# Turning q and k of the second batch on TensorE in a top-k attention + MLP kernel, where they were turned by DMA

## The chip, the cores and the metric

The kernel runs on one core of one Trainium2 chip. The metric is device time in microseconds, from the start of the program to its end; smaller is better. A measurement is the median of several runs.

## What is computed

Attention over 8 batches of 8 heads, 576 rows of 64 values each, in float32, in which every row keeps only its 32 largest scores; then a two-layer MLP with a sigmoid-gated activation on the result. Cut to what matters:

```python
# q, k, v: (8, 8, 576, 64)
scores = (1 / sqrt(64)) * q @ k.T                  # (576, 576) for each head
kth = np.partition(scores, -32)[..., -32:-31]
scores = np.where(scores >= kth, scores, -1e9)
attn = softmax(scores)                             # over the kept ones
attn_out = attn @ v                                # (8, 8, 576, 64)
x = attn_out.transpose(0, 2, 1, 3).reshape(4608, 512)
h = x @ w_in                                       # (4608, 2048)
g = h * sigmoid(1.702 * h)
out = g @ w_out                                    # (4608, 512)
```

## The kernel before

**Slots.** The unit of attention work is a slot: 128 query rows of a pair of heads (`hp`, 0 to 3). A head has 576 = 4 x 128 + 64 rows, so a batch has 16 full slots, and two more ("ends") that put the last 64 rows of two head pairs together: 18 slots a batch, 144 in all. Slots 0 to 17 are batch 0; slot 18 is the first of batch 1, which the kernel's text calls `b == 1` and this document "the second batch". Slots 18, 19, 20 and 21 are the first to need the q and k of its head pairs 0, 1, 2 and 3.

**What one slot does.** TensorE computes the scores (`scores`, L283). ScalarE copies them scaled from PSUM to SBUF (`copy_scores`, L295). VectorE pairs the two halves of each row (`pair_up`, L324; GpSimd makes the complement, L327 and L328), and finds the 32nd largest (`topk_of_pairs`, max and match-replace, L345 and L348): this document calls it "the find". GpSimd forms a bound (`lows`, L378). ScalarE applies the threshold (L398) and the exponential (L401). The probabilities must then be turned, and this is done by DMA: ScalarE splits the float32 words into their two 16-bit halves (`split`, L471), a DMA writes them to DRAM (L473), and a transposing DMA brings them back turned (`turn_by_dma`, L479, tile `pt`). TensorE multiplies with v (`values_at`, L539), ScalarE copies the result out of PSUM (L921) and GpSimd divides by the sum of the row (`x_of`, L553), which TensorE has turned (`sum_rows`, L528).

**The MLP beside it.** As soon as the four head pairs of 128 rows are done, the rows are appended to `ready`. Four hidden steps (`hidden`, L587, 32 matmuls each), each with a tanh on ScalarE (L604) and a gate on GpSimd (L616, L617), and four projection steps (`project`, L635, 8 matmuls each) make the output of 128 rows; ScalarE takes it from PSUM (L641, tile `ob`) and a DMA stores it. A projection of the next rows needs `ob` to have been read out. Tanh results and `ob` share five buffers.

**What sets the order.** Nothing is scheduled by a planner: the program order is written by hand, each engine executes its part of it strictly in order, and semaphores between the engines come from the tiles. Slots 0 to 12 are issued by `slot(n)`; from slot 13 on `two_slots(n)` issues two slots at a time, n = 13, 15, 17 and so on ("pair 13", "pair 15"). Work that is due at a slot is entered by `at(slot, function, arguments)` (L682 to L686) and taken up there: loads and v at the beginning of each half of a pair (`begin`), preparations of q and k at a fixed place in each half (`prepare_some`, L898 and L936). SyncE's queue (SP) issues nearly all DMAs, also in program order: a DMA that waits for its data holds up all that follow it.

In pair n, TensorE's order is: a hidden step and a projection (if there is something to do), then at L902 the turned sums of slots n-3 and n-2, scores of n+2, values of n-3 and n-2, scores of n+3 (in pair 13 the first of these come at other places), then a second hidden step and projection. ScalarE's order is: exponentials and split of slot n-1; tanh; scores of n+2; the first half of the exponentials of n, the copy L921, the second half; split of n; scores of n+3; tanh; `ob` where due. VectorE does the finds of n and n+1. The find of slot n contains, after 14 of its steps, `pair_up(n+1)`, which needs the copied scores of n+1.

**How q and k get turned.** q and k are loaded with rows on partitions (`load_both`: six DMAs to a tile `qk_l`, two buffers) and are needed with the 64 values of a head on partitions (tile `qk_t`, six buffers). There are two ways in the kernel:

- `prepare` (L210), used for batch 0: for q, four 128 x 128 transposes on TensorE (L218) into one PSUM bank (tile `tp`, two buffers, which the hidden steps and the results of `values_at` use in turn too), and a ScalarE copy of 128 x 512 (L219); for k the same, and one more transpose for the 64 last rows of both (L222) with three ScalarE copies of 128 x 64 (L223, L225).
- `prepare_by_dma` (L236), used for batches 1 to 7: a ScalarE copy that splits all words into 16-bit halves (L241, 128 x 2304; the tile `halves` takes a buffer of the probabilities' pool), four DMAs that write them to DRAM (L245, twice, L249, L250), and a transposing DMA (L254) that brings them back. That last one isn't issued at once: it is put into the list `turns`, which `two_slots` works off just behind `turn_by_dma(n - 1)` (L911).

Where the second batch is fetched and prepared is set by two tables, counted from slot 18:

```python
    READY_1 = (-5, -4, -2, -1)      # slots 13, 14, 16, 17
    FETCH_1 = (-11, -9, -4, -3)     # slots 7, 9, 14, 15
```

Of the kernel before, what the change touches and what calls it, by code (L numbers as in the profile page):

```python
# [30 lines left out]
def kernel(  # L31
# [238 lines left out]
    PER = N // B  # L270
    st = [{} for _ in slots]

    def scores(n):
        b, t, hps = slots[n]
        ps = [ps_s.tile([P, 2, 512], F32, name="s_ps") for _ in range(2)]
        if t < NF:
            parts = [(i, 0, slice(0, P), slice(t * P, (t + 1) * P)) for i in range(2)]
        else:
            parts = [(i, p, slice(p * TAIL, (p + 1) * TAIL), slice(FULL, S)) for i, p in ((0, 0), (1, 1), (0, 1), (1, 0))]
        for c in range(2):  # L280
            for i, p, rows, cols in parts:
                on = slice(i * D, (i + 1) * D)
                nc.tensor.matmul(  # L283
                    ps[i][rows, c, 0:HALF],
                    lhsT=qT[b, hps[p]][on, cols],
                    rhs=kT[b, hps[p]][on, FIRST[i] + c * HALF : FIRST[i] + (c + 1) * HALF],
                )
        st[n]["ps"] = ps
# [93 lines left out]
    def bounds(n):  # L382

        if n >= PAIRED:
            return lows(n)
        top = st[n]["top"]
        cut = st[n]["cut"] = small.tile([P, 2], F32, name="cut")
        low = st[n]["low"] = small.tile([P, 2], F32, name="low")
        nc.gpsimd.tensor_scalar(cut[:], top[:, :, TOPK - 1], -1.0, None, op0=ALU.mult)  # L389
        nc.gpsimd.tensor_tensor(out=low[:], in0=top[:, :, TOPK - 1], in1=top[:, :, 0], op=ALU.subtract)  # L390
# [34 lines left out]
    def invert(n):  # L425

        k = n // 2
        if k in sums:
            total = sums[k][:]
            nc.vector.tensor_scalar_add(total, total, 1e-9)  # L430
            inverse = small.tile([P, 4], F32, name="inverse")
            nc.vector.reciprocal(inverse[:], total.rearrange("p s j -> p (s j)"))
            wide = sums[k] = raws.tile([P, 2, 2, D], F32, name="wide", tag="raw")
            nc.gpsimd.tensor_copy(
                out=wide[:].rearrange("p s j d -> p (s j) d"),
                in_=inverse[:].unsqueeze(2).to_broadcast([P, 4, D]),
            )
# [29 lines left out]
    def split(n):  # L467

        pr, sc = st[n]["pr"], st[n]["sc"]
        halves = sc[:].rearrange("p i k -> p (i k)").bitcast(U16).rearrange("p (h k) -> p h k", h=2)  # L470
        nc.scalar.copy(out=halves, in_=pr[:].bitcast(U16).rearrange("p (k h) -> p h k", h=2))  # L471
        rows = st[n]["rows"] = apart.tile([P, 2, 2 * S], U16, name="rows")
        nc.sync.dma_start(rows[:], halves)  # L473
# [137 lines left out]
    def gate(aside):  # L611
        if not gated:
            return
        th, h, g, rows = gated.pop(0)
        if aside:
            nc.gpsimd.tensor_scalar(th[:], th[:], 1.0, 1.0, op0=ALU.add, op1=ALU.mult)  # L616
            nc.gpsimd.tensor_tensor(out=th[:], in0=th[:], in1=h[:], op=ALU.mult)  # L617
        else:
            nc.vector.scalar_tensor_tensor(
                out=th[:], in0=th[:], scalar=1.0, in1=h[:], op0=ALU.add, op1=ALU.mult  # L620
            )
        to_project.append((th, g, rows))

    def project(put_off_leaving=False):

        gT, fs, rows = to_project.pop(0)
        if fs.start == 0:
            pos[:] = [
                home.tile([P, C], F32, name="po", tag=tag) for home, tag in ((ps_p, "po"), (ps_h, "ph"))[: len(rows)]
            ]  # L630
        blocks = iter(range(G))
        for f in fs:
            for po in pos:
                i = next(blocks)
                nc.tensor.matmul(  # L635
                    po[:], lhsT=gT[:, i * P : (i + 1) * P], rhs=wout[:, f, :], start=(f == 0), stop=(f == FC - 1)
                )
        if fs.stop == FC:
            def leave(po, to_rows):
                ob = thp.tile([P, C], F32, name="ob", tag="th")  # L640
                nc.scalar.mul(out=ob[:], in_=po[:], mul=0.5 / RAISE**2)  # L641
                for on, to in to_rows:
                    nc.sync.dma_start(to, ob[on, :])

            leaving.extend(lambda po=po, to=to: leave(po, to) for po, to in zip(pos, rows))
            if not put_off_leaving:
                leave_all()
# [10 lines left out]
    def at(n, fn, *args):  # L658
        later.setdefault(n, []).append((fn, args))
# [2 lines left out]


    READY = (-13, -11, -5, -3)
    READY_1 = (-5, -4, -2, -1)
    FETCH = (-17, -15, -9, -7)
    FETCH_1 = (-11, -9, -4, -3)
    VALUES = (0, 1, 2, 3)
    by_slot = dict(enumerate([2, 2, 3, 3, 3, 3, 3, 3, 3, 3, 2, 2]))
    for n in by_slot:  # L670
# [11 lines left out]
    for b in range(1, B):  # L682
        for hp in range(NP):
            at(b * PER + (FETCH if b > 1 else FETCH_1)[hp], load_both, b, hp)
            at(b * PER + (READY if b > 1 else READY_1)[hp], prepare_by_dma, b, hp)
            at(b * PER + VALUES[hp], load_v, b, hp)  # L686
    unfinished = []
    early = []
# [2 lines left out]
    def finish_one():  # L691
        unfinished.pop(0)()

    def may_project(waiting):

        return len(to_project) > waiting and len(finished) >= NG * CC + to_project[0][1].stop
# [62 lines left out]
    def bring_all():  # L759

        waiting = len(ready)
        while put_off:
            put_off.pop(0)()
        if len(ready) > waiting:
            hidden()
# [83 lines left out]
    def two_slots(n):  # L849

        first, second = [later.pop(m, []) for m in (n, n + 1)]
        live = lambda m: 0 <= m < N
        aside = n < N

        def begin(todo):
            for fn, args in todo:
                if fn is not prepare_by_dma:
                    fn(*args)

        def prepare_some(todo):  # L860
            for fn, args in todo:
                if fn is prepare_by_dma:
                    fn(*args)

        def find(m):
            for i, op in enumerate(topk_of_pairs(m) if live(m) else [lambda: None] * 23):
                op()
                if i == 8 and m % 2:
                    invert(m - 2)
                if i > 1 and unfinished:  # L870
                    finish_one()

        def project_one():
            if may_project(0):
                project(True)

        def measure(m):
            if live(m):
                bounds(m)
            gate(aside)  # L880

        opens = n == SETTLED + 1
        begin(first)
        measure(n - 1)
        if opens:
            scores(n + 2)
            bring_all()
        if live(n - 1):
            exponentials(n - 1)
            split(n - 1)  # L890
        if opens:
            copy_scores(n + 2)
            tanh(aside)
        find(n)
        hidden(ps_t if opens else None)
        project_one()
        tanh(aside)
        prepare_some(first)  # L898
        held = [m for m in (n - 3, n - 2) if live(m) and "rows" in st[m]]
        o = ps_t.tile([P, 2, 2, P], F32, name="o", tag="tp") if held else None  # L900
        for i, m in enumerate(held):
            sum_rows(m, o[:, i, 0, :])  # L902
        if live(n + 2) and not opens:
            scores(n + 2)
            copy_scores(n + 2)
        leave_all()
        for i, m in enumerate(held):
            values_at(m, o[:, i, 1, :])
        if live(n - 1):
            turn_by_dma(n - 1)  # L910
        while turns:  # L911
            turns.pop(0)()
        if live(n + 3):
            scores(n + 3)
        begin(second)
        measure(n)
        def bring():
            if not held:
                return
            x = raws.tile([P, 2, 2, P], F32, name="x", tag="raw")  # L920
            nc.scalar.copy(out=x[:], in_=o[:])  # L921
            for i, m in enumerate(held):
                x_of(m, x[:, i, 1, :], x[:, i, 0, :])

        if live(n):
            exponentials(n, bring)
        else:
            bring()
        if live(n):
            split(n)  # L930
            turn_by_dma(n)
        hidden(ps_t)
        if live(n + 3):
            copy_scores(n + 3)
        tanh(aside)
        prepare_some(second)  # L936
        project_one()
        leave_all()
        find(n + 1)
# [41 lines left out]
```

## Time and profile before

| | |
|---|---|
| median of 3 runs | 1498.21 us (1497.76 to 1498.99) |
| the profiled execution | 1497.24 us, of which the span from the first to the last instruction is 1495.4 us |
| TensorE matmul busy | 1441.8 us, 96% of the span |
| VectorE busy | 1384.7 us, 93% |
| ScalarE busy | 1176.5 us, 79% |
| GpSimd busy | 858.8 us, 57% |
| mean granted TensorE clock | 0.983 |

In the profile PE is TensorE's matmuls, PEld its weight loads, DVE is VectorE, ACT ScalarE, POOL GpSimd, SPq the queue of SyncE. `out<-in` names tiles, L283 a line of the kernel. The page cuts the span into 40 slices of 37.4 us and gives the busy share of each in tenths; PEclk is the clock that TensorE was granted. A wait is put down to the operation that ended last. The chain of waits is followed back from the last instruction: what each step had to wait for. A stretch table gives busy times between two points of time; the timeline gives the instructions of an engine in order. TensorE's matmuls overlap each other, so their listed duration is more than the distance from one to the next.

### The profile page before, as it was taken

What the parts mean: (1) busy time and instruction counts of PE and PEld (TensorE: products, weight loads), DVE (VectorE), ACT (ScalarE), POOL (GpSimd) and SP (SyncE); (2) the same over time, 40 slices, a digit from 0 to 9 for tenths busy, and PEclk for the clock granted to TensorE, in tenths of its full rate; (3) what the DMA queues carried; (4) which work ended last, traced back from release to release, by engine and by line L of the source; (5) the groups of instructions that cost most, each with busy time, mean ns of one, the idle gap of its engine ahead of it and who ended that gap; (6) DMA issues with size and microseconds to landing.
All of it is one profiled execution on the core that took longest, in us unless ns stands there. A gap on an engine that the chain in (4) does not pass through costs nothing.

```text
span 1495.4 us, 31374 instructions
## 1 busy us (share of the span) xinstructions
PE 1441.8 (96%) x10748; PEld 1053.6 (70%) x10748; DVE 1384.7 (93%) x4541; ACT 1176.5 (79%) x1849; POOL 858.8 (57%) x1119
## 2 busy tenths in 40 slices
PE   7789968999999999999999999999999999999998
PEld 5667735777777777777777777777777777777775
DVE  7999987999999999999999999999999999999910
ACT  7998666888878787888878787888878888777730
POOL 3887534666665665556655556666665556656510
PEclk8999978999999999999999999999999999999999
DMA  8450378766767586766767767786867767544430
GB/s 247 143 160 30 81 209 199 186 183 183 179 184 190 158 201 174 191 183 164 180 177 198 178 180 176 183 197 165 191 171 186 188 179 174 153 131 124 133 87 15
DMA packets 531298, 247.17 MB, mean 165 GB/s; under 512 B 462784, under 2 KB 505537, under 8 KB 531137
## 3 DMA queue, kind: packets, MB, share of 16 engines
q1 hardware_dynamic: 530704, 244.87, 63.0%
q8 instruction: 84, 1.38, 0.4%
q14 instruction: 78, 0.63, 0.1%
q10 hardware_dynamic: 432, 0.30, 0.1%
HBM read 45.09 MB, written 104.73 MB: 100 GB/s over the span
## 4 chain that ended last, share of the span: by engine, by line
PE 89%; DVE 7%; DMA 2%; ACT 1%; SPq 1%; issue 0%; POOL 0%; ACTq 0%; POOLq 0%
PE ph L587 34%; PE po L635 33%; PE o L539 10%; PE s_ps L283 10%; DVE top L305 3%; DVE left L308 2%; PE o L528 1%; DMA pt<-rows 1%; PE tp L449 1%; DMA rows<-sc 0%; DMA qk_t<-qk_rows 0%; DVE win L153 0%; PE o L504 0%; ACT pr L401 0%; PE none L170 0%
## 5 line engine op out<-in xcount | busy, mean ns | idle before, releaser
L635 PE MATMUL po<-wout,th 128*128 128x512 f32 x1152 | 521.8, 596 | 2.8 <-ACT ob L641 2.8
L587 PEld LDWEIGHTS ph<-xT,win 128*128 128x128 f32 x4096 | 472.2, 192 | 54.4 <-issue 52.6
L587 PE MATMUL ph<-xT,win 128*128 128x128 f32 x4096 | 484.7, 277 | 0.4 <-ACT xT L517 0.4
L635 PEld LDWEIGHTS po<-wout,th 128*128 128x128 f32 x1152 | 209.3, 192 | 215.3 <-issue 211.2
L345 DVE MAX8 top<-left 128x8 f32<-128x288 f32 x792 | 325.5, 446 | 0.0
L471 ACT COPY sc<-pr 128x2304 uint16<-128x2304 uint16 x132 | 278.8, 2112 | 4.2
L295 ACT ACTIVATE sc<-s_ps 128x576 f32<-128x576 f32 x288 | 170.9, 646 | 139.9 <-PE s_ps L283 136.0
L348 DVE MATCH_REPLACE8 left<-top,left 128x288 f32<-128x288 f32 x528 | 229.7, 443 | 0.0
L328 POOL TENSOR_TENSOR lesser<-lesser,greater 128x576 int32<-128x576 int32 x132 | 186.6, 1414 | 62.4 <-DVE greater L324 57.1
L401 ACT ACTIVATE pr<-sc,low 128x576 f32<-128x576 f32 x288 | 221.4, 778 | 0.0
L345 DVE MAX8 top<-lesser 128x8 f32<-128x288 f32 x528 | 213.6, 445 | 0.0
L398 ACT ACTIVATE sc<-sc,cut 128x576 f32<-128x576 f32 x288 | 208.1, 778 | 5.5 <-POOL cut L389 5.1
L283 PE MATMUL s_ps<-qk_t 64*128 64x288 f32 (+1 forms) x1280 | 184.6, 436 | 10.2 <-DMA qk_t<-qk_rows 9.9
L327 POOL TENSOR_TENSOR lesser<-sc 128x576 int32<-128x576 int32 x132 | 186.9, 1416 | 10.6 <-ACT sc L295 10.6
L553 POOL TENSOR_TENSOR xT<-x 128x128 f32<-128x128 f32 x116 | 50.7, 458 | 235.8 <-ACT x L921 198.6
L617 POOL TENSOR_TENSOR th<-th,h 128x512 f32<-128x512 f32 x128 | 162.9, 1272 | 10.7
L324 DVE TENSOR_TENSOR greater<-sc 128x576 f32<-128x576 f32 x132 | 141.0, 1068 | 20.9 <-ACT sc L295 14.6
L539 PE MATMUL o<-pt,v_l 128*64 128x128 f32 (+1 forms) x2368 | 145.4, 267 | 9.4 <-DMA pt<-rows 9.4
L539 PEld LDWEIGHTS o<-pt,v_l 128*64 128x64 f32 x2368 | 121.2, 139 | 35.1 <-issue 23.7
L283 PEld LDWEIGHTS s_ps<-qk_t 64*128 64x128 f32 (+1 forms) x1280 | 100.5, 180 | 51.7 <-issue 34.0
L604 ACT ACTIVATE th<-ph 128x512 f32<-128x512 f32 x144 | 85.8, 596 | 58.7 <-PE ph L587 54.6
L616 POOL TENSOR_SCALAR th<-th 128x512 f32<-128x512 f32 x128 | 79.0, 617 | 92.0 <-ACT th L604 92.0
(86 smaller groups left out, 1593.2 us busy)
## 6 DMA issues: line engine op xcount, KB each, us to landing
rows<-sc SPq DMA_DIRECT2D x132, 576.0 KB, 3.2
qk_rows<-halves SPq DMA_DIRECT2D x56, 256.0 KB, 2.8
qk_l<-in_q_dram SPq DMA_DIRECT2D x64, 128.0 KB, 3.0
raw<-in_moe_w_in_dram SPq DMA_DIRECT2D x16, 512.0 KB, 4.6
v_l<-in_v_dram SPq DMA_DIRECT2D x32, 256.0 KB, 3.1
raw<-in_moe_w_out_dram SPq DMA_DIRECT2D x16, 512.0 KB, 3.6
out_dram<-ob SPq DMA_DIRECT2D x32, 256.0 KB, 2.9
qk_l<-in_k_dram SPq DMA_DIRECT2D x62, 128.0 KB, 2.9
```

The costliest lines, as they stand in the source:

```text
L283: nc.tensor.matmul(ps[i][rows, c, 0:HALF], lhsT=qT[b, hps[p]][on, cols], rhs=kT[b, hps[p]][on, FIRST[i] + c * HALF : FIRST[i] + (c + 1) * ...
L295: nc.scalar.mul(out=to, in_=ps[i][:, :, 0:HALF], mul=SCALE)
L327: nc.gpsimd.tensor_tensor(out=whole, in0=a.bitcast(I32), in1=b.bitcast(I32), op=ALU.add)
L328: nc.gpsimd.tensor_tensor(out=whole, in0=whole, in1=greater[n][:].bitcast(I32), op=ALU.subtract)
L345: nc.vector.max(found(r, i, True), src[:, i, :])
L348: nc.vector.match_replace(to[:, i, :], found(r, i), src[:, i, :], LOWEST)
L398: nc.scalar.activation(sc[:, i, :], sc[:, i, :], AF.Prelu, bias=cut[:, i : i + 1], alpha=HUGE)
L401: nc.scalar.activation(pr[:, i * S : (i + 1) * S], sc[:, i, :], AF.Exp, bias=low[:, i : i + 1], accum_out=den[:, i : i + 1],)
L471: nc.scalar.copy(out=halves, in_=pr[:].bitcast(U16).rearrange("p (k h) -> p h k", h=2))
L539: nc.tensor.matmul(o[j * D : (j + 1) * D, cols], lhsT=main[:, j, c, :] if c < NF else tail[:, j, :], rhs=pt[:, MAIN[j] + c if c < NF else ...
L587: nc.tensor.matmul(ph[:, i * tiles * P : (i + 1) * tiles * P], lhsT=win[:, c, f * P : (f + 1) * P], rhs=xT[c], start=(c == 0), stop=(c == ...
L635: nc.tensor.matmul(po[:], lhsT=gT[:, i * P : (i + 1) * P], rhs=wout[:, f, :], start=(f == 0), stop=(f == FC - 1))
```

## The change

The second batch's head pairs are prepared by `prepare` instead of `prepare_by_dma`, once with "q" and once with "k", at the first half of pairs 13, 15, 17 and 19 (slots 13, 15, 17, 19, where they were prepared at 13, 14, 16 and 17). The fetch of its last head pair is entered at slot 16 instead of 15. In `two_slots` the two helper functions know `prepare` as a preparation. Batches 2 to 7 stay as they are.

```diff
-    READY_1 = (-5, -4, -2, -1)
+    READY_1 = (-5, -3, -1, 1)
     FETCH = (-17, -15, -9, -7)
-    FETCH_1 = (-11, -9, -4, -3)
+    FETCH_1 = (-11, -9, -4, -2)
...
             at(b * PER + (FETCH if b > 1 else FETCH_1)[hp], load_both, b, hp)
-            at(b * PER + (READY if b > 1 else READY_1)[hp], prepare_by_dma, b, hp)
+            if b > 1:
+                at(b * PER + READY[hp], prepare_by_dma, b, hp)
+            for name in "qk" if b == 1 else "":
+                at(b * PER + READY_1[hp], prepare, name, b, hp)
...
         def begin(todo):
             for fn, args in todo:
-                if fn is not prepare_by_dma:
+                if fn is not prepare and fn is not prepare_by_dma:
                     fn(*args)
 
         def prepare_some(todo):
             for fn, args in todo:
-                if fn is prepare_by_dma:
+                if fn is prepare or fn is prepare_by_dma:
                     fn(*args)
```

## The prediction

> **What bounds the kernel now.** I read the slices of the page first, to see where an engine stands still.
>
> ```profile
> PE   7789968999999999999999999999999999999998
> DVE  7999987999999999999999999999999999999910
> PEclk8999978999999999999999999999999999999999
> ```
>
> From slice 8 on (262 us) PE is at 9 in tenths at full clock. The hole is in slices 6 and 7, 187 to 262 us, at a lower clock too. The stretch table beside two later pairs (columns: stretch, length, busy us and count of PE, PEld, DVE, ACT, POOL, then PEclk, DMA share, GB/s):
>
> ```profile
> 172.40:242.00 69.60, 47.59 (x278) 28.96 (x278) 53.05 (x179) 48.30 (x65) 27.87 (x38) 0.80 0.78 195
> 242.00:261.10 19.10, 19.10 (x139) 13.92 (x138) 18.82 (x66) 15.20 (x24) 10.26 (x14) 1.00 0.74 196
> ```
>
> A later pair takes 19.10 us and PE is busy for all of it: PE is the bound there, DVE nearly so. Between 172.4 and 242.0 PE stands idle for 69.60 - 47.59 = 22.0 us, at clock 0.80. Its waits there, and DVE's longest (columns: total, times, longest):
>
> ```profile
> PE s_ps L283 <- DMA qk_t<-qk_rows: 9.9, 1, 9.9
> PE o L539 <- DMA pt<-rows: 9.4, 2, 6.0
> PE po L635 <- ACT ob L641: 2.8, 1, 2.8
> ...
> DVE greater L324 <- ACT sc L295: 14.6, 5, 8.4
> ```
>
> These are the whole 22. The chain of waits, cut to this stretch, shows who lies behind them:
>
> ```profile
> 188.86 3.25 DMA rows<-sc
> 192.16 4.42 DMA pt<-rows
> ...
> 205.52 2.00 ACT halves L241
> 207.52 0.51 ACT ob L641
> 208.02 0.04 issue
> 208.07 5.15 PE po L635 x8
> 213.22 6.16 DMA pt<-rows
> ...
> 225.97 5.59 DMA qk_t<-qk_rows
> 231.56 0.14 issue
> 231.69 2.29 PE s_ps L283 x8
> ```
>
> SP is the hidden culprit. SP's waits list the four halves DMAs once held up by ScalarE for 8.9 us (L245 behind L241, until 175.64). Behind them in the queue stood turn_by_dma(12), the turn of (1,0), six loads and, ready since 180.61 but issued at 188.86, the rows of slot 13; so pt came at 196.6. Later eight halves DMAs (215.85 to 223.2) stand ahead of turn_by_dma(16) and the two last qk_t turns (225.97, 228.7); scores(20), and behind it all of PE, waited for the first.
>
> **What the skill says.** "TensorE: Matmul & The Clock Gate", Part 4 (PE-mode transpose): about 275 ns for one transpose in a kernel, into PSUM, so that a copy must follow. The opening's own transposes agree:
>
> ```profile
> L218 PE MATMUL tp<-ident,qk_l x24: 272/273/472, 8.6 to 21.4; 128*128 128x128 f32 x24
> L219 ACT COPY qk_t<-tp x6: 571/590/603, 9.2 to 25.2; 128x512 f32<-128x512 f32 x6
> ```
>
> In the timeline eight of them take 1.04 us from the first's start to the last's end: 0.13 apart. The same page, Part 1: TensorE falls to half clock after an idle window of about 3.4 us. The trace agrees: eight score matmuls take 1.24 us at full clock, and 2.29 after the 9.9 us wait. "Advanced Engine Details and Errata", X-Bar Transpose, has transposing DMAs as fast as regular ones (350 to 400 GB/s). Here it isn't so: a qk_t turn moves 1216 x 512 bytes, 0.62 MB, in 5.1 us from issue to landing, 122 GB/s. "SBUF — State Buffer", Who interferes with whom: a VectorE tensor_tensor with both inputs in SBUF and a GpSimd instruction block each other. The trace has L324 at 0.74 us and, in alternate finds, at 1.42.
>
> **The change, part by part.** I follow the work up to one mark, the start of L528 in pair 19, 242.00 now. There the last of the four new preparations is over.
>
> Removed: four ScalarE splits of 2.12 us; 16 halves DMAs and four turns on SP, by the queue's rows (2 x 0.5 + 0.53 + 0.66 + 2.9) about 5.1 us of SP for each head pair, 20 in all. None of it is on PE. All three DMA waits lose their cause or come earlier. Pool order is otherwise untouched: four uses fewer of the probabilities' two buffers is an even number.
>
> Added for each head pair: 9 transposes on PE, 9 x 0.13 = 1.2 us (upper end 9 x 0.275 = 2.5), and on ScalarE 2 x 0.54 + about 0.45 = 1.5 us (9.20 to 10.65 in the opening), which is 0.5 less than the split. New waits: the fifth k transpose needs q's PSUM buffer copied out, the following `o` needs k's. Behind the waiting transpose on PE stand the sums, scores and values of the same pair; behind ScalarE's copies stand copy_scores and, through it, VectorE's L324.
>
> Pair 13 (1,0). PE's projection ends at 172.43. ScalarE's tanh and copy of `ph`, which k's buffer needs, end at 173.6 as now. So q turns at 172.5, k at 173.65, the ends at 174.2; scores(16) at 174.5, 2.0 later than now (1.2 work, 0.8 wait). ScalarE is through at 175.35, now 175.50: nothing changes for exponentials(13) and copy_scores(16). SP: turn_by_dma(12) goes at 169.6 (rows landed), now 177.97; the six loads of (1,2), which wait for the buffer of (1,0), at 174.6 to 179.7, now 183.78 to 188.86; rows(13) at 180.5; pt(13) lands about 188.2, now 196.6.
>
> Pair 15 (1,1), moved from slot 14. PE: hidden and projection to 189.85 (two us late). ScalarE's next tanh waits for that projection, as its buffer does now, and ends with its copy at 190.95; q's copy 191.5, k's 192.0, so L528 at 192.05, now 187.72. scores(17) end at 193.5 and are copied by 194.7, now 193.38: this is a loss of 1.3 for VectorE, whose find(16) then ends at 198.2, now 196.94. But values(13) start without their 6.0 us wait and at full clock: both values to 195.2, scores(18) to 196.4, now 201.18. From here everything is early. split(15) ends at 200.3 (now 203.3), copy_scores(18) at 201.4 (205.5), so find(17) has no wait: it ends at 207.5, now 209.46. The fetch of (1,3), moved past rows(14) and its turn, occupies SP from 197.0 to 202.1, ahead of rows(15), which costs that 1.8 us (ready 200.3); pt(15) lands about 210, and is wanted at 211. Cover enough by 1 us; without it, that much more wait in pair 17.
>
> Pair 17 (1,2), moved from slot 16. `ob` is read at 202.0 (now 207.9), the projection runs to 205.6; split(16) ends at 207.0 (now 213.0), then q's and k's copies; L528 at 208.1, now 213.30. scores(20) no longer wait for a DMA, but only for values(15): 212.4, now 231.69. find(18) ends at 216.4 (219.78), split(17) at 216.8 (226.1), copy_scores(20) at 217.9 (235.2), so find(19) has no wait either and ends at 225.7, now 240.1: VectorE is 14.4 ahead.
>
> Pair 19 (1,3), moved from slot 17. Two projections to 220.7. The new late thing is ScalarE: exponentials(18) and split(18) end at 222.9 (from 217.8, 1.44 + 1.6 + 2.1), then q 223.4, k 223.9, and L528 at 224.0. PE's own work would have been ready 2.1 us before.
>
> I add 1.5 us for some nine handovers between PE and ACT that I set nearly to nothing (0.16 us each is what the opening's L283 waits after L219): mark at 225.5, 16.5 earlier. The following hidden step waits 0.5 us more for its x than now. Net 16. Check by addition: 22.0 idle plus 8.5 slow clock (47.59 busy against 39.1 for the same instructions at full clock) are 30.5; back come 36 x 0.13 = 4.7 work, waits 0.8 + 1.0 + 2.05 (`ob`) + 1.3 + 2.1 = 7.3, and the 2.0 of handovers and x: 16.5 remain.
>
> After the mark PE is the bound at 19.1 a pair, and nothing in pairs 21 on is changed, so the 16 stay to the end; DVE, 14.4 ahead where PE is 16 ahead, loses 2 of its lead. Its first sum (L430) of a pair precedes L528 by 8.7 now, so there is room.
>
> The profiled execution is 1497.24 (span 1495.4 and 1.8 around it): 1481.2. The median of the runs lies 1.0 above it: **1482.2**.
>
> **Rivals.**
> *Half of it refilled* (14%): the copies of `prepare` queue behind exponentials and split (5.1 us) in three pairs, PE idles past its 3.4 us window and slows. Price 3 x 2.7 more: gain 8, 1490. For it: the opening's L222 waited 3.69 and 1.57 us for L219. Against: ScalarE had rounding of weights ahead of it there.
> *Larger* (6%): handovers cost nothing, and the `ob` wait hides: gain 21, 1477.
> *The wait is hidden anyway* (4%): pt<-rows stays late, because rows and turns (3.2 + 4.7 us) still run through SP, and scores(20) find the next wait at once. Time within 3 us of 1498. Against: SP is free of 20 us.
> *Slower* (8%): a steady pair depends on the phase of VectorE against GpSimd. In a pair one L324 takes 1.42 instead of 0.74, and L430 0.34 at the median instead of 0.15; VectorE's free time is then 18.82 - 0.68 - 0.19 = 17.95. With VectorE 2 us later against PE, both L324 and L430 could hit GpSimd: 17.95 + 1.36 + 0.85 = 20.2. It decides from 19.1 on. Half way between, 19.6, costs 0.5 in each of the 60 pairs, 30 us, net 1512. Against: a later VectorE normally catches up by 1.1 a pair when it meets nothing.
>
> **Numbers.** Likeliest: 1482 (68%, 1478 to 1487). Range 1476 to 1491: it takes most of the half case and of the larger one, the upper transpose cost (2.5 instead of 1.2, four times, 5 us: 1487) inside. Within 0.2% (3 us, about what a measurement can tell from none): 4%, slower 8%, faster 88%.
>
> **What would show it.** Right: no wait for qk_t before 250 us; pt waits in pair 15 gone; L528 of pair 19 near 225; pairs of 19.1 us after it; PE waits for ACT of 1 to 2 us at L222 or L528 four times. Wrong: any of the 60 later pairs longer, or L528 of pair 17 not before 213. The prediction fails as a whole if ScalarE's order makes scores(17) later than 195, as find(16) then passes on every us.

## The result, and the profile after

The changed kernel takes 1482.80 us (median of 4 runs, 1482.14 to 1483.86), the kernel before 1498.60 in the runs beside it (4 runs, 1497.76 to 1499.13). The ratio is 0.9896, with a 95% interval of 0.9879 to 0.9913: 1% faster. The forecast was 1482.2. The profiled execution took 1482.51 us, with a span of 1480.7.

The page's slices after:

```profile
PE   7789899999999999999999999999999999999998
DVE  7999989999999999999999999999999999999920
PEclk8899999999999999999999999999999999999999
```

The hole of TensorE in slices 6 and 7 is gone, and so are its low digits of the clock. TensorE's waits after, from 150 to 262 us (columns: total, times, longest):

```profile
PE tp L222 <- ACT qk_t L219: 4.6, 3, 3.0
PE tp L449 <- POOL by L414: 3.3, 1, 3.3
PE po L635 <- ACT ob L641: 1.1, 1, 1.1
PE o L528 <- ACT qk_t L219: 0.8, 3, 0.3
PE tp L218 <- ACT h L607: 0.7, 1, 0.7
```

No DMA is among them any more: the 9.9 us for qk_t and the 9.4 us for pt have left the list. The line with L449 lies before the change (slot 12). What is left, 4.6 + 1.1 + 0.8 + 0.7 = 7.2 us, is TensorE waiting for ScalarE.

To see where the time went I cut both traces at the same instructions: the start of the projection of slot 12 (156.85 us before, 158.51 after), the start of L528 in pair 21, which is the first pair at the steady pace (261.10 and 247.12), and the same in the last steady pair (1388.62 and 1374.65). The stretch tables, before:

```profile
156.85:261.10 104.25, 82.24 (x504) 53.59 (x503) 87.32 (x297) 71.30 (x103) 45.32 (x61) 0.87 0.67 174
261.10:1388.62 1127.52, 1127.52 (x8495) 820.74 (x8494) 1111.27 (x3777) 929.34 (x1410) 682.57 (x898) 1.00 0.69 177
```

And after:

```profile
158.51:247.12 88.61, 81.36 (x540) 54.53 (x539) 82.40 (x287) 68.84 (x119) 43.83 (x58) 0.98 0.54 149
247.12:1374.65 1127.53, 1127.53 (x8496) 820.70 (x8495) 1111.32 (x3776) 932.72 (x1410) 682.93 (x897) 1.00 0.69 177
```

| part | before | after | difference |
|---|---|---|---|
| opening, slots 0 to 12 | 156.85 | 158.51 | +1.66 |
| slot 12 to pair 21 | 104.25 | 88.61 | -15.64 |
| steady pairs | 1127.52 | 1127.53 | +0.01 |
| end | 106.78 | 106.05 | -0.73 |
| span | 1495.4 | 1480.7 | -14.7 |

The whole gain lies in the second row. There TensorE's idle time falls from 104.25 - 82.24 = 22.01 us to 88.61 - 81.36 = 7.25. Its busy time falls too, by 0.88, though 36 transposes have been added. From the first transpose of a preparation to the matmul behind the last one, less the waits, TensorE's timeline gives 1.35, 1.36, 1.37 and 1.37 us, 5.4 in all, so by this estimate about 6.3 us less went into slow clock. The steady pairs take the same time to a hundredth of a microsecond, and give nothing back. The opening has the same instructions in both kernels. In the 14 profiled executions of this study its end lies between 156.8 and 159.5 us; the profiled execution before was among the two shortest, which probably is why the profiles differ by less (14.7 us) than the medians (15.8).

### The profile page after: what moved, and what is told of

It is laid out like the page before. It is cut to its first block, busy times and chain, and to the rows that moved or that the text cites. A ratio compares the mean times of both kernels' runs of the same rounds, so it can differ in the third digit from the quotient of the medians.

```text
span 1480.7 us, 31436 instructions
## 1 busy us (share of the span) xinstructions
PE 1442.7 (97%) x10784; PEld 1056.0 (71%) x10784; DVE 1382.9 (93%) x4541; ACT 1177.6 (80%) x1865; POOL 859.2 (58%) x1119
## 4 chain that ended last, share of the span: by engine, by line
PE 88%; DVE 10%; ACT 2%; issue 0%; POOL 0%; POOLq 0%; ACTq 0%; DVEq 0%
PE ph L587 34%; PE po L635 32%; PE o L539 10%; PE s_ps L283 10%; DVE top L305 4%; DVE left L308 3%; PE o L528 1%; DVE top L345 1%; PE tp L449 1%; DVE wout L153 0%; DVE left L348 0%; PE none L170 0%; DVE greater L324 0%; ACT pr L401 0%; DVE win L153 0%
## 5 line engine op out<-in xcount | busy, mean ns | idle before, releaser
L635 PE MATMUL po<-wout,th 128*128 128x512 f32 x1152 | 518.6, 593 | 1.1 <-ACT ob L641 1.1
L635 PEld LDWEIGHTS po<-wout,th 128*128 128x128 f32 x1152 | 208.0, 190 | 211.0 <-issue 208.5
L327 POOL TENSOR_TENSOR lesser<-sc 128x576 int32<-128x576 int32 x132 | 187.0, 1417 | 2.4 <-ACT sc L295 2.4
L378 POOL TENSOR_SCALAR low<-cut,top 128x1 f32<-128x1 f32 x264 | 65.7, 265 | 175.6 <-DVE cut L357 174.1
L324 DVE TENSOR_TENSOR greater<-sc 128x576 f32<-128x576 f32 x132 | 153.8, 1165 | 11.7 <-ACT sc L295 5.5
L348 DVE MATCH_REPLACE8 left<-top,greater 128x288 f32<-128x288 f32 x264 | 114.7, 442 | 0.0
```

The source lines that it names most:

```text
L327: nc.gpsimd.tensor_tensor(out=whole, in0=a.bitcast(I32), in1=b.bitcast(I32), op=ALU.add)
L348: nc.vector.match_replace(to[:, i, :], found(r, i), src[:, i, :], LOWEST)
L635: nc.tensor.matmul(po[:], lhsT=gT[:, i * P : (i + 1) * P], rhs=wout[:, f, :], start=(f == 0), stop=(f == FC - 1))
```

## The experiments

All were timed beside the kernel before; the ratio is to that. The changed kernel's is 0.9896.

| kernel | us | ratio (95% interval) |
|---|---|---|
| first two head pairs on TensorE | 1489.69 | 0.9945 (0.9930 to 0.9960) |
| last two on TensorE | 1486.05 | 0.9919 (0.9904 to 0.9933) |
| old way beside the new | 1507.66 | 1.0062 (1.0045 to 1.0079) |
| split alone beside it | 1494.95 | 0.9982 (0.9975 to 0.9989) |
| not turned | 1479.79 | 0.9878 (0.9863 to 0.9893) |
| last head pair at slot 18 | 1483.13 | 0.9898 (0.9883 to 0.9913) |
| last two earlier | 1486.00 | 0.9919 (0.9905 to 0.9934) |
| changed kernel again | 1482.89 | 0.9898 (0.9881 to 0.9914) |
| old way beside, second version | 1496.93 | 0.9990 (0.9982 to 0.9998) |
| DMAs alone beside it | 1492.04 | 0.9957 (0.9944 to 0.9971) |
| not turned, constant written early | 1476.86 | 0.9850 (0.9836 to 0.9863) |
| copies first | 1481.86 | 0.9888 (0.9874 to 0.9901) |

### Half of the change at a time

```diff
 # first two on TensorE, the others by DMA
-    READY_1 = (-5, -3, -1, 1)
+    READY_1 = (-5, -3, -2, -1)
...
+            elif hp > 1:
+                at(b * PER + READY_1[hp], prepare_by_dma, b, hp)
-            for name in "qk" if b == 1 else "":
+            for name in "qk" if b == 1 and hp < 2 else "":
```

The other kernel has `READY_1 = (-5, -4, -1, 1)` and the two conditions the other way round.

> Head pairs 0 and 1 of the second batch on TensorE, 2 and 3 by DMA as before. Theory (two separate gains: SP's queue is no longer held up, so pt of slot 13 is in time, and scores(20) no longer wait for a qk_t turn): the 6.0 us wait for pt in pair 15 is gone; the halves and turns of head pairs 2 and 3 stand behind rows(16) and turn_by_dma(16), qk_t of (1,2) lands near 221 us, where the changed kernel computes scores(20) at 213.6; PE waits 7 us there and then runs slow: about 1491 us. Rival (only the direct wait for qk_t counts): no gain, 1497 to 1498.

> Head pairs 0 and 1 of the second batch by DMA as before, 2 and 3 on TensorE. Theory (two separate gains): the 6.0 us wait for pt in pair 15 and its slow clock stay, which is 3 to 5 us on the path after subtraction of what TensorE's transposes cost; no wait for qk_t: about 1487.5 us. Rival (only the direct wait for qk_t counts): the full gain, 1483.

With the first two on TensorE, 1489.69 us. TensorE's timeline:

```profile
213.66 0.39 PE L539 MATMUL o<-pt,v_e 128*64 128x128 f32 x4
225.19 2.29 PE L283 MATMUL s_ps<-qk_t 64*128 64x288 f32 x8 [11.14 <-DMA qk_t<-qk_rows]
227.41 7.93 PE L635 MATMUL po<-wout,th 128*128 128x512 f32 x16
```

Pair 15 no longer waits for pt. The wait of scores(20) for qk_t, in brackets, is as large as ever (11.1 us, expected 7), followed by matmuls at half pace. With the last two on TensorE, 1486.05 us:

```profile
195.81 1.12 PE L539 MATMUL o<-pt,v_l 128*64 128x64 f32 x16 [5.32 <-DMA pt<-rows]
...
216.76 1.09 PE L539 MATMUL o<-pt,v_l 128*64 128x128 f32 x16 [2.41 <-DMA pt<-rows]
```

Here it is the other way round: pt of slot 13 is late by 5.3 us, that of slot 15 by 2.4, and no qk_t is waited for. So both waits are real and have the two causes named; each half of the change takes away its own. The rival, that only the direct wait for qk_t counts, expected no gain in the first kernel and the full gain in the second. It falls clearly in the first, and in the second by 3 us (runs of 1484.4 to 1487.0 us, where the changed kernel's reach 1483.9 at most). The two gains (8.4 and 12.0 us in their own comparisons) add to more than the 15.8 of both together: a time that one wait no longer takes is partly taken by the next limit. The last transpose of pair 19 (L222) is an instance: it waits 1.8 us for ScalarE with the last two alone on TensorE, and 3.0 us in the changed kernel.

### What ScalarE's split costs, and the old way beside the new one

```diff
+    def split_only(b, hp):
+        t = loaded[b, hp]
+        halves = prp.tile([P, 2 * NF + 1, 2, P], U16, name="halves", tag="pr")
+        words = t[:].rearrange("p c j d -> p c (j d)").bitcast(U16)
+        nc.scalar.copy(out=halves[:], in_=words.rearrange("p c (e h) -> p c h e", h=2))
...
+            if b == 1:
+                at(b * PER + READY_1[hp], split_only, b, hp)
             for name in "qk" if b == 1 else "":
                 at(b * PER + READY_1[hp], prepare, name, b, hp)
```

> The changed kernel, with ScalarE's old split (2.12 us each) done as well, its result unused and not transferred. Theory (ScalarE's relief of 0.6 us each time isn't what brought the gain): up to 2.1 us more wait on PE in each of four pairs, some of it under other waits: about 1489 us. Rival (the relief of ScalarE is the gain): the gain is lost entirely, 1497 to 1500.

1494.95 us: 12 us more than the changed kernel, where 8.5 us of ScalarE's time (4 x 2.12) were added. My size was wrong by half, for a reason that TensorE's timeline shows:

```profile
238.41 0.48 PE L222 MATMUL tp<-ident,qk_l 128*128 128x128 f32 x1 [3.82 <-ACT qk_t L219]
239.00 0.66 PE L535 MATMUL o<-ident,wide 128*128 128x128 f32 x2
239.58 2.29 PE L290 MATMUL s_ps<-qk_t 64*128 64x288 f32 x8
241.81 1.97 PE L546 MATMUL o<-pt,v_l 128*64 128x128 f32 x16
```

The wait itself grew by what was added or less, to 2.8, 2.9 and 3.8 us in pairs 15, 17 and 19. But after each of these three, the next matmuls run at half pace: 2.29 us for scores that take 1.24, 1.97 for values that take 1.09. In the stretch from slot 12 to pair 21 the clock is 0.90 here and 0.98 in the changed kernel. ScalarE is thus on the path in these pairs, and work on it costs more than its length.

The rival's 1497 to 1500 lies nearer than my 1489, but this kernel doesn't give ScalarE the old load. It has the old split on top of the new copies, 8.5 us more than the changed kernel, where the kernel before has 2.5 us more from slot 12 to pair 21 (71.30 against 68.84 us busy). And none of its waits is for pt or qk_t, as the old ones were. At 1.4 us for each microsecond (12 for 8.5), ScalarE's relief would be worth an estimated 3.5 of the 15.8 us; it wasn't tried alone.

The old way was then left in whole beside the new one (split, four DMAs, turn), its result unused. The first version put the first two turned results into the tile that slot 16's scores still read, so these were computed from other data.

```diff
+        def turn():
+            nc.sync.dma_start_transpose(
+                out=whole[0, 2 + hp // 2][:].bitcast(U16),      # second version: whole[0, hp // 2 * 2]
+                in_=rows[0 : 2 * S + TAIL, :, :].rearrange("c h e -> (c h) e"),
+            )
```

> The changed kernel, with the old way left in beside it for all four head pairs: ScalarE's split, the four DMAs and the turn are all issued at the preparation's place, but the turned result is put into a tile that nobody reads. Theory (SP's queue is half of the gain): the wait for pt in pair 15 returns with 4 to 6 us, those in pair 17 in part, and ScalarE's 2.1 us each time add to the waits of L222: about 1494 us. Rival (only the direct wait for qk_t counts): no more than ScalarE's own 2.1 us each time, the same as with the split alone, near 1489. Rival (contention of transfers): the waits grow without a queue that is held up, all DMAs land late.

1507.66 us, outside of what either theory gave. Its waits show an error of the experiment: scores(16) waited 9.1 us for the turned tile (`PE s_ps L310 <- DMA qk_t<-qk_rows`), since they read what it overwrote. It says nothing on the question, except what one more such wait costs. The second version:

> As the old way beside the new one above, but the unused turned results go to tiles that no later scores read: there, the first ones went to the tile that scores(16) read, which waited for the turn. Theory: the split's own price (1495 us with the split alone) hides most of SP's hold-up, as TensorE wants pt of slot 13 some 5 us later than in the changed kernel; the rest, rows and turns behind 20 us of additional queue, costs 1 to 5 us: 1496 to 1500 us. Rival (contention of transfers, all land late): the 1507.7 us of the first version stay.

1496.93 us as expected, and no wait for qk_t, nor for pt before pair 21 (0.5 us there): TensorE's waits are those of the split alone (the last transpose, L223 in this kernel, behind ScalarE: 11.4 us in four). Contention of transfers as the explanation of 1507.7 falls. But it couldn't show what SP's part is, because the split hides it.

### SP's part alone

```diff
+    def dmas_unused(b, hp):
+        words = ident[:].bitcast(U16).unsqueeze(1).to_broadcast([P, 2 * NF + 1, 2 * P])
+        rows = apart_qk.tile([2 * (S + TAIL), 2, P], U16, name="qk_rows")
...
+        for g in range(2):
+            nc.sync.dma_start(
+                main[g].rearrange("(t p) w -> p t w", p=P), words[:, g * NF : (g + 1) * NF, :]
+            )
...
```

The two smaller DMAs and the turn to an unused tile follow as in the kernel above.

> The changed kernel with the old way's 16 DMAs to DRAM and four turns issued beside it, from a constant tile, so that they wait for nothing, their result unused: SP's 20 us of issue and the traffic come back, but neither ScalarE's split nor a wait behind it. Theory (SP matters because it is held up by a wait for ScalarE, and because scores wait for its last link, not because it is full): 0 to 3 us more than the changed kernel, 1483 to 1486. Rival (SP's occupation or the DMA traffic itself made the old way slow): most of the 15.8 us come back, 1493 or more.

1492.04 us, 0.61% or 9.1 us more than the changed kernel. By SP's timeline the DMAs added here take 24 us of its queue, where the old ones took 22 in the kernel before. My theory gave 0 to 3 and was wrong here; the rival's 1493 is nearer. TensorE's waits for pt are back:

```profile
PE o L562 <- DMA pt<-rows: 8.9, 3, 4.3
```

Pair 17 shows how (SP's timeline of this kernel, whose slot 12 lies within 0.02 us of the changed kernel's):

```profile
196.68 2.56 SPq L502 DMA_TRANSPOSE pt<-rows  x1
199.41 2.66 SPq L278 DMA_TRANSPOSE qk_t<-qk_rows  x1
...
206.15 0.54 SPq L496 DMA_DIRECT2D rows<-sc  x1
209.41 2.54 SPq L502 DMA_TRANSPOSE pt<-rows  x1
```

and the same three in the changed kernel:

```profile
196.69 2.25 SPq L479 DMA_TRANSPOSE pt<-rows  x1
...
202.96 0.59 SPq L473 DMA_DIRECT2D rows<-sc  x1
206.26 2.30 SPq L479 DMA_TRANSPOSE pt<-rows  x1
```

One turn of 2.7 us between them puts rows(15), and the issue of pt(15), 3.2 us later. In the changed kernel pt(15) landed some 1.6 us before TensorE took it up (206.26 + 4.6 against 212.44); here it was taken up at 215.53, 6.1 us after its issue, so 1.5 us of the delay are a slower transfer. The wait should then be 3.2 + 1.5 - 1.6 = 3.1 us; the trace has 2.9. The next two waits are 1.7 us in pair 19 and 4.3 in pair 21. Over these pairs pt lands 5.0 us after its issue at the median, 4.6 in the changed kernel: most of the delay is the queue, some the traffic, and the two were not tried apart. So it isn't only ScalarE holding up SP: SP has no time to give in these pairs.

### What the preparation still costs

```diff
+    def not_turned(b, hp):
+        both = new_pair(b, hp)
+        loaded.pop((b, hp))
+        nc.gpsimd.memset(both[:], 0.01)
```

It stands in place of `prepare`; the second batch's scores come from this constant.

> The changed kernel without any turning of q and k of the second batch: their tiles are filled with a constant by one GpSimd instruction each, so the second batch is computed from constants. It prices what the preparation still costs. Theory (PE's 4.7 us of transposes, some 6 us of waits for ScalarE's copies and 1.7 us of slow clock in pair 19 are what is left): about 8 to 10 us less than the changed kernel, 1474 us. Rival (VectorE's finds set the pace of pairs 15 to 19 anyway): within 3 us of the changed kernel, 1480 to 1483.

1479.79 us, where 1474 was expected. The constant was late itself: TensorE waited 3.9 us for it in pair 19, so the price was understated. The second version writes it at the beginning of the pair.

> As the kernel without turning above, but GpSimd's constant is written at the beginning of each half of a pair, since in that run scores(21) waited 3.9 us for it in pair 19. The second batch is computed from constants. Theory (VectorE's finds are the next bound, all of its waits in pairs 13 to 17 but 0.6 us are gone there already): 1476 to 1479 us, VectorE without waits and PE waiting for it. Rival (PE's waits are still the bound): 4 us less and more, below 1475.5.

1476.86 us, 6 us less than the changed kernel, inside the expected range. VectorE has one wait of 0.6 us left from 165 to 262 us, and TensorE's longest wait is for what GpSimd makes of VectorE's sums (`wide`):

```profile
PE o L534 <- POOL wide L440: 2.4, 1, 2.4
PE o L545 <- DMA pt<-rows: 1.8, 2, 1.1
PE po L641 <- ACT ob L647: 1.1, 1, 1.1
```

From slot 12 to pair 21 this takes 81.44 us, of which VectorE is busy for 80.07. So a preparation that costs TensorE and ScalarE nothing gains 7 us on the 88.61 of the changed kernel's first profile. That VectorE's finds are the next bound is argued from this one wait of 2.4 us; its busy share alone doesn't show it (see the last section).

### Attempts to get some of that

```diff
-    READY_1 = (-5, -3, -1, 1)
+    READY_1 = (-5, -3, -1, 0)     # last head pair at slot 18
+    READY_1 = (-5, -3, -2, 0)     # and the third at slot 16
```

> The changed kernel, with the last head pair prepared one slot earlier (slot 18, second half of pair 17, where ScalarE waits 1.0 us for VectorE anyway, instead of slot 19, behind the split of slot 18). Theory: the 3.0 us wait of L222 in pair 19 and the 1.7 us of slow clock that follow it go: 4 us less than the changed kernel, 1479 us. Rival (something else, VectorE or the copy of x, is as late): within 1 us of the changed kernel.

> As the one before, and head pair 2 at slot 16 (second half of pair 15) instead of 17. Theory: the 0.9 us wait of L222 in pair 17 goes, but ob, which the next projection waits for, now stands behind 1.5 us of copies: between 1 us less and 1 us more than with head pair 3 alone, about 1479 us.

1483.13 and 1486.00 us: the first the same as the changed kernel, the second 3 us slower. The reason, in the timeline of the first:

```profile
215.20 1.09 PE L218 MATMUL tp<-ident,qk_l 128*128 128x128 f32 x8
220.07 0.33 PE L222 MATMUL tp<-ident,qk_l 128*128 128x128 f32 x1 [3.78 <-ACT qk_t L219]
220.24 8.73 PE L635 MATMUL po<-wout,th 128*128 128x512 f32 x16
```

TensorE comes to the transposes earlier, while ScalarE is still at the exponentials and the split of slot 17; the wait is 3.8 us instead of 3.0, and it now stands ahead of two projections that would have filled the time (8.73 us at slow clock, 7.13 in the changed kernel). I had looked at where ScalarE was free and not at where TensorE was early. In the second kernel the same happens in pair 15 too (3.7 us). The other way out, the second head pair at slot 14, wasn't tried. By the program's order, ScalarE's tanh would there wait for a projection that stands behind the transposes on TensorE, and these would wait for the tanh to give a PSUM buffer free, so that the program would not end.

> The changed kernel again, unaltered, beside the three others on the same chip: 1482.8 us within 1 us. It also shows how much the untouched opening, before 150 us, varies from one profiled execution to the next (1.66 us between the two at hand).

1482.89 us; from slot 12 to pair 21 it took 87.15 us in this profile, 88.61 in the other. TensorE's waits are the same in both, 7.25 us. What differs is the clock behind the longest of them. Pair 19 in the first profile:

```profile
225.78 0.33 PE L222 MATMUL tp<-ident,qk_l 128*128 128x128 f32 x1 [2.97 <-ACT qk_t L219]
...
226.70 1.82 PE L283 MATMUL s_ps<-qk_t 64*128 64x288 f32 x8
228.46 1.98 PE L539 MATMUL o<-pt,v_l 128*64 128x128 f32 x16
```

and in this one:

```profile
226.65 0.33 PE L222 MATMUL tp<-ident,qk_l 128*128 128x128 f32 x1 [2.97 <-ACT qk_t L219]
...
227.57 1.24 PE L283 MATMUL s_ps<-qk_t 64*128 64x288 f32 x8
228.74 1.09 PE L539 MATMUL o<-pt,v_l 128*64 128x128 f32 x16
```

The same wait of the same program was followed by a slow clock in one execution and by a full one in the other. Its length alone doesn't decide: in the kernel with the first two on TensorE, a wait of 3.1 us for `ob` was followed by full pace (8 matmuls of L635 in 3.70 us).

The last attempt moves ScalarE's copies ahead of the split:

```diff
             exponentials(n - 1)
+            if n in (17, 19):
+                prepare_some(first)
             split(n - 1)
...
-            ends = ps_t.tile([P, 512], F32, name="tp")
+            apart = b == 1 and hp > 1
+            ends = (ps_h if apart else ps_t).tile([P, 512], F32, name="ph" if apart else "tp")
```

> The changed kernel, with the preparations of head pairs 2 and 3 moved ahead of the split of slots 16 and 18 in the program (same slots 17 and 19), and their fifth k transpose in the hidden step's PSUM bank, which is idle then: ScalarE's copies no longer stand behind 2.1 us of split, and the transpose no longer waits for q's copy. Theory: L528 of pair 19 comes 2 to 3 us earlier, the wait of L222 (3.0 us) and the slow clock after it go: 1479 to 1480 us. Rival (the moved copies delay split and rows, and a later wait takes it back, as with head pair 3 at slot 18): 1482 to 1484.

1481.86 us, ratio 0.9888 against 0.9896: no difference that these intervals can tell. The waits of L222 (L223 in this kernel) in pairs 17 and 19 are gone as meant, and two others have come. One of 2.3 us is for pt of slot 15: its values are reached 2.4 us earlier now, and its transfer took 5.9 us instead of 4.5. The scores behind this wait took 2.27 us. The other, 1.6 us, is for GpSimd's x in pair 19; the chain of waits leads from it back through ScalarE to the find of slot 19 on VectorE. From slot 12, L528 of pair 19 starts after 65.91 us instead of 67.85, and that of pair 21 after 87.10, as in the second profile of the changed kernel (87.15; 88.61 in the first). A later wait took the gain back, as the rival said, but not for its reason: the rows of slot 15 were issued as early as before (44.55 us after slot 12, against 44.45), and x hangs on VectorE.

## Why the prediction was right, point by point

To compare with the prediction, which counts from the trace before, 1.66 us are subtracted from the times after.

- *The order in pair 13 and 15.* scores(16) were to start at 174.5: 174.4. L528 of pair 15 at 192.05: 192.1. copy_scores(17) done at 194.7: 194.9, so VectorE lost time in find(16) as told (its wait grew from 2.75 to 4.62 us; 1.3 more was foretold). pt of slot 13 landed at 187.8 (188.2 foretold), and nobody waited.
- *Pair 17.* L528 at 208.1: 208.1. scores(20) at 212.4: 212.0, and they waited for no DMA.
- *Pair 19.* L528 at 225.5, with 1.5 us for handovers: 224.7. "PE's own work would have been ready 2.1 us before" was a wait of 3.0 + 0.25.
- *The sum.* Net 16 us; 15.64 measured in this stretch, 17.1 in the second profile of the changed kernel. All of it stayed to the end, as said. That the sum is so close is in part luck, as its terms were off in both directions (those foretold add to 16.5; the path, with 0.5 for x, gave 16):

| term | foretold | measured |
|---|---|---|
| idle time that goes | 22.0 | 22.0 |
| slow clock that goes | 8.5 | 6.3 (7.7 in the second profile) |
| 36 transposes | -4.7 | -5.4 |
| waits that come back | -7.3 | -7.25 |
| handovers and x | -2.0 | in the waits above |

- *The waits.* They were to be 0.8, 1.0, 2.05 (`ob`), 1.3 and 2.1 us, and were 0.73, 1.03, 1.13, 1.14 and 3.22. That they add to the same is chance. The handovers didn't come on top of them, and nobody waited for x.
- *The transposes.* Four take 0.60 us and eight 1.04, so they are 0.11 us apart. Each group ends with a full 0.27, and a wait begins a new group. The 0.13 was the 1.04 shared out over eight.
- *What was mis-sized.* The wait of pair 19 is one term. The other is the slow clock after it, which the sum set at nothing. The step from L528 of pair 19 to the next hidden step was to be 0.5 us longer than before, for x. It is 6.65 against 4.98 us in the first profile, 1.7 longer by slow clock alone, and 5.02 in the second. L528 itself came 0.8 earlier than foretold, so that in the first profile the two nearly cancel. This is the mechanism of the rival "half of it refilled", in one pair of three. The rival set the limit at 3.4 us of idleness; here shorter waits (2.8 us with the split beside, 2.3 with the copies first) were followed by half pace.
- *VectorE.* It was to be 14.4 us ahead after find(19) and is 12.5 (83.02 us from slot 12 to its last instruction before, 70.56 after). L324 took 1.45 and 1.90 us in find(17) and find(18), as it met GpSimd's L327, and ended 0.62 us after it both times: the block that the Trainium skill's "SBUF — State Buffer" (Who interferes with whom) names, here with two inputs from SBUF on VectorE. In pair 19 ScalarE waited 1.0 us for VectorE.
- *A reason that was said too weakly.* "SP is the hidden culprit" named ScalarE holding up SP. The DMAs alone show that the queue's own time (24 us in that kernel; 20 in the prediction), with the traffic, costs 9 us even without that. The prediction had the piece in one place (pt(15) with a cover of 1 us), and my expectation of 0 to 3 us didn't draw the conclusion.
- *A reason that was wrong.* Against the slower rival I said that a later VectorE catches up by 1.1 us a pair. It doesn't; see the last section. The pair didn't grow for it.

## What to carry to other kernels

A DMA path is priced by its place in the queue: every step of it stands before somebody's data, and the instruction that waits longest may belong to another transfer. When moving such work to a busy engine, add up the waits at the handovers; with the split beside, each microsecond more on ScalarE cost 1.4. Let the range hold a slow clock after TensorE waits of 2 to 4 us: here it followed most of them, but not all. And a place is free only if both engines of a handover get there together: to look where one is idle gained nothing in one kernel and cost 3 us in another.

## What the runs showed that I had not expected

VectorE's place against TensorE, once shifted, stays. Before, the first sum (L430) of a pair starts 8.7 to 9.1 us ahead of L528, after the change 5.4, from pair 21 (241.70 and 247.12) to the last (1369.29 and 1374.65), and the pair takes 19.1 us on average in both. What gives is L324 and L430. Their instructions in the steady stretch, before (columns: ns min/median/max, first and last start):

```profile
L430 DVE TENSOR_SCALAR sums<-sums x60: 153/342/519, 271.3 to 1398.9; 128x4 f32<-128x4 f32 x60
...
L324 DVE TENSOR_TENSOR greater<-sc x119: 732/759/1445, 264.3 to 1391.9; 128x576 f32<-128x576 f32 x119
```

and after:

```profile
L430 DVE TENSOR_SCALAR sums<-sums x59: 146/150/155, 280.0 to 1388.4; 128x4 f32<-128x4 f32 x59
...
L324 DVE TENSOR_TENSOR greater<-sc x120: 757/1062/1973, 263.2 to 1399.7; 128x576 f32<-128x576 f32 x120
```

L430 no longer meets anything (150 ns instead of 342), the longest L324 takes 1.97 us instead of 1.45. Busy time of VectorE in the steady stretch is the same, 1111 us: it is stretched to the length of the pair inside its instructions and shows no wait at all. By this reading a VectorE at 98.6% busy was not at its limit here, and how much slack it has can't be read from its busy time.
